# Attention and two feed-forward networks on one core: loads, conversion steps and attention in the order in which their data come, and the sigmoid ahead of the root

## The chip, the cores and the metric

One Trainium2 chip, of which the program uses one core. The metric is the device time of one execution in microseconds (us). Engines are called as the profile calls them: PE (TensorE, matrix products; PEld is its weight load), DVE (VectorE), ACT (ScalarE), POOL (GpSimd) and SP (SyncE, which here only issues transfers). All but PE's weight loads run their own instructions strictly in order, and wait for each other by semaphores.

## The reference

```python
kv  = np.einsum('bhsd,bhse->bhde', k, v)          # 4 batches, 8 heads, 576 rows, 64 wide
out = np.einsum('bhsd,bhde->bhse', q, kv)
rms = np.sqrt(np.mean(out * out, axis=-1, keepdims=True) + 1e-06)
x   = (out / rms * g_norm)                        # to 2304 x 512: tokens x (heads * 64)
gate = 1.0 / (1.0 + np.exp(-(x @ w_gate)))        # 512 x 1536
y   = (gate * (x @ w_val)) @ w_out                # 1536 x 512
h   = y @ w_in2                                   # 512 x 2048
out = (np.maximum(h, 0.0) + np.log1p(np.exp(-np.abs(h)))) @ w_out2   # 2048 x 512
```

q, k, v and g_norm are float32; the five weight matrices are float64.

## The kernel before

**Products.** A large product runs as three passes in the type float32r: both operands are split into a high and a low part, and high by high, high by low and low by high are summed in PSUM (`mm3`). So each operand needs its high part (a cast on ACT, `split_hi`, L67) and its low part (a subtraction on DVE, `split_lo`, L70), and the passes with the low parts come last.

**Stages.** The tokens are cut into five tiles of 512, 512, 384, 384 and 512. The first FFN takes tile after tile, and in each tile 12 steps of 128 columns of the hidden width: chain "g" (x by w_gate into `ps_g`), sigmoid on ACT into `sg` (`sigmoid`), chain "v" (x by w_val into `ps_v`), the gating `sg * ps_v` on DVE (`gated`), its high part on ACT and its low part on DVE (`ghl`), and the output chain of the step before into `yacc`. The second FFN takes the five tiles again, 16 steps each: `ps_h`, a softplus in pieces on ACT and DVE (`e`, `u`, `ln`, `ghl2`), and the output chain two steps later into `oacc`. The y between the two is written out and loaded again, and split for the second FFN by `y_split`.

**Attention.** For tile 0 it stands ahead of everything, one pair of heads (hp 0 to 3) after another: `kv_mm`, the transposed q (`qt_mm`), `o_mm`, the sum of squares (`o_square`), root and reciprocal (`o_root`), scaling (`o_scale`), transposition (`xt_mm`), and the split of x (`xt_split`). For tile 1 the same pieces lie in steps 2 to 8 of tile 0, and for tiles 2 to 4 (the piece being up to 256 tokens: `q_trans`, `po_mm`, `ss_mm`, `rms_root`, `rms_scale`) in the steps of the tile ahead.

**Weights.** They come as pairs of 32-bit words in loads of 512 KB; two units (a unit is what one step needs of one matrix) make an item of 1 MB. Item 0 is gate and value of step 0, item 1 the output units of steps 0 and 1, item 2 gate and value of step 1, item 3 those of step 2, item 4 the output units of steps 2 and 3, and so on: 18 items for the first FFN, 16 for the second. Each item is made into float32r by four operations: A (`conv_a`, two passes on ACT, L141 and L143), B (`conv_b`, two on DVE, L150 and L153), H (`conv_h`, ACT, L67) and L (`conv_l`, DVE, L70). `conv_step` issues H, A, B and L of up to four different items, if there is something for each; `conv_to(done)` repeats it until so many items have had L; `conv_target(n)` gives that number for each step. Items of the second FFN are loaded in the last tile of the first one, into blocks that its finished steps give free (`prefetch`); the scratch tiles of attention (`scratch`) lie in the blocks of the last seven items of the first FFN, which so can be loaded only when attention for tile 1 is done with them.

**Order.** Nothing is scheduled by a planner: the code's own order is the order of each engine. A step of the first FFN has places, at which the pieces of attention are put by a table: chain "g"; "A"; gating of the step before; "a"; its low part; "bg"; a third of the conversion; the sigmoid; chain "v"; "B"; a third; "b"; a third; the output chain; "C", "c", "late". All loads are issued by SP, at most eight under way at a time, so that a load waits there both for its place and for its block.

```python
        if ph == 1:
            done = n_l[0]
            step = max(0, conv_target(n) - done)
...
            run("bg")
...
            conv_to(done + (step + 2) // 3)
            sigmoid(t, i)
            ffn1_mm(t, i, "v", range(3 if n == 0 else 0, KD))
```

Of the kernel before, what the change touches and what calls it, by code (L numbers as in the profile page):

```python
# [8 lines left out]
F32 = mybir.dt.float32  # L9
# [20 lines left out]
def attention_moe_moe_kernel(ctx: ExitStack, tc: tile.TileContext, q, k, v, g_norm,  # L30
# [141 lines left out]

    def conv_step():
# [35 lines left out]
    QROWS, KV, QT, SQ, ON, KVF = 0, 2, (7, 8), 9, (10, 11), 12  # L211
# [398 lines left out]
    two = (nc.sync, nc.scalar)  # L610
    load_kv(0, 0, two)
# [4 lines left out]
    for hh in range(2):  # L616
        nc.scalar.dma_start(out=g_col[64 * hh:64 * hh + 64, :], in_=g_norm.rearrange("(d o) -> d o", o=1))
    load_kv(0, 2)
    load_q_rows(0, 2)
    load_item()  # L620
    load_kv(0, 3)
    load_q_rows(0, 3)

    def a_in(hp):
        kv_mm(0, hp)
        qt_mm(0, hp, MM)
        kv_evac(0, hp)
# [19 lines left out]
    conv_a()
    a_out(2)
    conv_b()
    a_x(1)  # L650
    conv_h()
    for _ in range(3):
        load_item()
    for part in (0, "rest", 1, 2, 3):
        load_kv(1, part)
    load_item()
    load_item()
    a_out(3)
    conv_l()
    for c in "gv":  # L660
        ffn1_mm(0, 0, c, (0,))
    conv_a()
    a_x(2)
    for c in "gv":
        ffn1_mm(0, 0, c, (1,))
    conv_b()
    a_x(3)
    for c in "gv":
        ffn1_mm(0, 0, c, (2,))
    conv_step()  # L670
# [17 lines left out]
    def call(f, *a):  # L688
        return lambda: f(*a)
# [60 lines left out]
    for n in range(len(its) + LAG2):  # L750
# [15 lines left out]
        if ph == 1:  # L766
# [6 lines left out]
            gate_lo_prev()  # L773
            run("bg")
# [10 lines left out]
        elif ph == 2:  # L785
# [10 lines left out]
            if n_l[0] < len(items):  # L796
                conv_step()
# [63 lines left out]
```

## Time and profile before

| | before |
|---|---|
| median of three runs | 960.85 us (960.76 to 962.49) |
| the profiled execution | 963.4 us |
| its span in the profile | 961.6 us |
| mean granted TensorE clock | 0.982 |
| busy: PE, PEld | 918.1 us (95%), 785.0 us (82%) |
| busy: DVE, ACT, POOL | 550.5 us (57%), 456.2 us (47%), 1.6 us (0%) |

The busy times are averages over stages that differ. A granted clock of 1.0 is 2.4 GHz, one of 0.5 is 1.2 GHz, at which a matmul takes twice as long. The span is the profiled execution from its first instruction to its last, and the difference to its time lies around it.

### The profile page before, as it was taken

To read this page: it belongs to the slowest core of one execution; us is meant where nothing else is said; L and a number is where in the kernel's file an instruction comes from. 1 tells how busy PE (TensorE), PEld (TensorE's weight loads), DVE (VectorE), ACT (ScalarE), POOL (GpSimd) and SP (SyncE) were. 2 spreads that over 40 slices of the span, in tenths; PEclk is the share of its full clock that TensorE was granted. 3 is DMA by queue.
4 is the path that set the end of the run, shared out by engine and by line. 5 is a ranking of instruction groups with operands and counts; after the bars stand their busy time and mean duration, and the time that the engine had idled before them with its cause. 6 is when DMAs were issued, how large, how long until landed. Compare 5 with 4: busy or idle time off the path is not lost.

```text
span 961.6 us, 11999 instructions
## 1 busy us (share of the span) xinstructions
PE 918.1 (95%) x4685; PEld 785.0 (82%) x4685; DVE 550.5 (57%) x909; ACT 456.2 (47%) x784; POOL 1.6 (0%) x8
## 2 busy tenths in 40 slices
PE   7489999999999999999989999999999999999998
PEld 6267778878898999999867768888888999998886
DVE  2656675343455534555676675566566566566554
ACT  3555755332335334442656654454445445454443
POOL 0000000000000000000000000000000000000000
PEclk9789989999999999999999999999999999999999
DMA  9760511321011302000645520002001102000001
GB/s 304 229 234 20 200 53 46 99 62 20 0 49 43 92 3 56 22 22 1 220 163 175 175 88 1 1 0 77 1 1 33 45 1 78 1 1 33 1 1 44
DMA packets 72137, 64.75 MB, mean 67 GB/s; under 512 B 30352, under 2 KB 63120, under 8 KB 72080
## 3 DMA queue, kind: packets, MB, share of 16 engines
q1 hardware_dynamic: 70848, 63.33, 21.1%
q10 hardware_dynamic: 1232, 0.66, 0.3%
q8 instruction: 37, 0.61, 0.3%
q14 instruction: 20, 0.16, 0.1%
HBM read 54.53 MB, written 9.44 MB: 67 GB/s over the span
## 4 chain that ended last, share of the span: by engine, by line
PE 80%; DMA 7%; DVE 6%; ACT 4%; issue 2%; SPq 1%; DVEq 0%; ACTq 0%
PE oacc L63 21%; PE ps_h L63 20%; PE ps_g L63 12%; PE ps_v L63 12%; PE yacc L63 11%; DMA w_raw<-in_moe_w_in_dram 2%; DVE w_raw L150 2%; DVE w L70 1%; DMA kv_raw<-in_k_dram 1%; DVE w L153 1%; DMA w_raw<-in_moe_w_gate_dram 1%; DMA kv_raw<-in_v_dram 1%; ACT w_raw L143 1%; PE kv_ps L255 1%; ACT w_raw L141 1%
## 5 line engine op out<-in xcount | busy, mean ns | idle before, releaser
L63 PE MATMUL oacc<-w,ghl 128*128 128x512 f32 x864 | 210.4, 391 | 0.0
L63 PE MATMUL ps_g<-x,w 128*128 128x512 f32 (+1 forms) x720 | 167.6, 380 | 26.2 <-ACT sg L479 13.4
L63 PEld LDWEIGHTS oacc<-w,ghl 128*128 128x128 f32 x864 | 161.5, 188 | 32.9 <-DVE ghl L70 0.8
L63 PEld LDWEIGHTS ps_g<-x,w 128*128 128x128 f32 x720 | 133.4, 193 | 49.2 <-ACT sg L479 16.0
L63 PE MATMUL ps_v<-x,w 128*128 128x512 f32 (+1 forms) x720 | 162.7, 374 | 5.9 <-DVE sg L485 5.9
L63 PE MATMUL yacc<-ghl,w 128*128 128x512 f32 (+1 forms) x720 | 161.9, 373 | 2.1 <-ACT ghl L67 1.9
L63 PEld LDWEIGHTS ps_v<-x,w 128*128 128x128 f32 x720 | 131.1, 190 | 25.5 <-DVE sg L485 8.3
L63 PEld LDWEIGHTS yacc<-ghl,w 128*128 128x128 f32 x720 | 130.8, 189 | 20.2 <-ACT ghl L67 2.3
L551 ACT ACTIVATE e<-ps_h 128x512 f32<-128x512 f32 (+1 forms) x80 | 44.4, 556 | 199.4 <-PE ps_h L63 190.2
L63 PE MATMUL ps_h<-y,w 128*128 128x512 f32 (+1 forms) x576 | 128.5, 372 | 0.3 <-ACT sg L479 0.3
L63 PEld LDWEIGHTS ps_h<-y,w 128*128 128x128 f32 x576 | 106.1, 188 | 17.1 <-ACT sg L479 0.7
L560 DVE TENSOR_SCALAR u<-e 128x512 f32<-128x512 f32 (+1 forms) x80 | 32.0, 400 | 149.4 <-ACT e L552 149.4
L63 PE MATMUL ps_h<-y_odd,w 128*128 128x512 f32 (+1 forms) x384 | 82.4, 363 | 0.0
L67 ACT CAST ghl<-sg 128x512 fp32r<-128x512 f32 (+1 forms) x60 | 34.6, 577 | 98.5 <-DVE sg L485 98.3
L63 PEld LDWEIGHTS ps_h<-y_odd,w 128*128 128x128 f32 x384 | 70.2, 188 | 8.9
L70 DVE TENSOR_TENSOR ghl<-sg,ghl 128x512 fp32r<-128x512 f32 (+1 forms) x60 | 38.2, 636 | 29.4 <-ACT ghl L67 29.2
L562 DVE SCALAR_TENSOR_TENSOR e<-ps_h,e 128x512 f32<-128x512 f32 (+1 forms) x80 | 51.0, 638 | 2.8
L569 DVE TENSOR_TENSOR e<-e,u 128x512 f32<-128x512 f32 (+1 forms) x80 | 51.0, 638 | 2.8
L70 DVE TENSOR_TENSOR ghl<-e,ghl 128x512 fp32r<-128x512 f32 (+1 forms) x80 | 50.3, 628 | 0.7 <-ACT ghl L67 0.7
L568 DVE SCALAR_TENSOR_TENSOR u<-u,ln 128x512 f32<-128x512 f32 (+1 forms) x80 | 50.5, 631 | 0.0
L150 DVE SCALAR_TENSOR_TENSOR w_raw<-w_raw 128x1024 uint32<-128x1024 uint32 x34 | 41.5, 1221 | 15.4 <-ACT w_raw L143 15.4
L485 DVE TENSOR_TENSOR sg<-sg,ps_v 128x512 f32<-128x512 f32 (+1 forms) x60 | 37.8, 629 | 20.3 <-PE ps_v L63 12.4
(87 smaller groups left out, 765.6 us busy)
## 6 DMA issues: line engine op xcount, KB each, us to landing
w_raw<-in_moe_w_out_dram SPq DMA_DIRECT2D x28, 512.0 KB, 4.7
w_raw<-in_moe_w_in_dram SPq DMA_DIRECT2D x16, 512.0 KB, 4.9
w_raw<-in_moe_w_gate_dram SPq DMA_DIRECT2D x12, 512.0 KB, 6.3
w_raw<-in_moe_w_val_dram SPq DMA_DIRECT2D x12, 512.0 KB, 7.7
out_dram<-ob SPq DMA_DIRECT2D x17, 256.0 KB, 2.4
kv_raw<-in_k_dram SPq DMA_DIRECT2D x16, 256.0 KB, 3.9
kv_raw<-in_v_dram SPq DMA_DIRECT2D x14, 256.0 KB, 4.2
y_dram<-ys SPq DMA_DIRECT2D x6, 512.0 KB, 2.8
```

The lines of the kernel that those rows point to most:

```text
L63: nc.tensor.matmul(out=ps, lhsT=lhs(a), rhs=rhs(b), start=start and n == 0, stop=stop and n == 2)
L67: nc.scalar.copy(out=hi, in_=src)
L70: nc.vector.tensor_tensor(out=lo, in0=src, in1=hi.bitcast(F32), op=ALU.subtract)
L141: nc.scalar.activation(out=hi.bitcast(F32), in_=hi.bitcast(F32), func=ACTF.Copy, scale=float(2.0 ** -112))
L143: nc.scalar.activation(out=lo, in_=lo, func=ACTF.Copy, bias=-0.5, scale=float(2.0 ** -29 * (1 - 2.0 ** -20)))
L150: nc.vector.scalar_tensor_tensor(out=lo, in0=hi, scalar=3, in1=lo, op0=ALU.logical_shift_left, op1=ALU.bitwise_or)
L485: nc.vector.tensor_tensor(out=sg, in0=sg, in1=chain.pop(("v", t, i)), op=ALU.mult)
L551: nc.scalar.activation(out=e, in_=ps, func=ACTF.Abs)
L560: nc.vector.tensor_scalar(out=u, in0=e, scalar1=1.0, scalar2=None, op0=ALU.add)
L562: nc.vector.scalar_tensor_tensor(out=e, in0=chain.pop(("p", t, i)), scalar=0.0, in1=e, op0=ALU.max, op1=ALU.add)
L568: nc.vector.scalar_tensor_tensor(out=u, in0=u, scalar=1.0, in1=ln, op0=ALU.subtract, op1=ALU.subtract)
L569: nc.vector.tensor_tensor(out=e, in0=e, in1=u, op=ALU.subtract)
```

## The change

- Item 0 is no longer converted as an item: its gate unit and its value unit are loaded, converted (A, B, H, L at half width, lines named `early_`) and used each by itself. In step 0 chain "v" stands whole behind chain "g", and no longer piece by piece beside it.
- Attention for tile 0 is issued in another order (`a_in`, `a_q`, `a_o`, `a_scale` and the transpositions apart). Items 1 to 5 are loaded ahead of k and v of batch 1, and g_norm by SP instead of ACT.
- Attention for tile 1 lies a step later in tile 0. The late loads are two in step 4, three in step 6, and two in step 9 at "bg". The scratch tiles lie in other blocks, and the last two items of the first FFN change places.
- How far the conversion goes in each step of tile 0 stands in two tables, `L_END` for L and `A_LIM` for A.
- In each step of the first FFN the first third of the conversion and the sigmoid stand ahead of "bg" (where the roots of attention are) and of `y_split`.
- In the last tile of the first FFN conversion goes one item a step and stays further behind the loads. In the second FFN what is left of it is done in every second step.
- The scalings behind a root are spread over other places, and the first piece of tile 3 lies a step later in parts.

```diff
+    for n in (n_first - 2, n_first - 1):
+        for (kind, f) in items[2 * n_first - 3 - n]:
+            block_of["gv" if kind in "gv" else "o", f] = n
+    items[-2:] = items[:-3:-1]
...
-        if na < n_load[0]:
+        if na < min(n_load[0], a_lim[0]):
             conv_a()
...
-    QROWS, KV, QT, SQ, ON, KVF = 0, 2, (7, 8), 9, (10, 11), 12
+    KV, SQ, QROWS, QT, KVF, ON = 0, 5, 6, (8, 9), 10, (12, 13)
...
+    a_in(0)
+    a_q(0)
...
+    early_a(0)
+    a_q(2)
+    xt_mm(0, 0, ACC)
+    a_scale(1)
+    early_b(0)
...
+    early_h(0)
+    xt_split(0, 1)
+    early_l(0)
+    a_o(3)
+    early_a(1)
+    ffn1_mm(0, 0, "g", (0,))
+    xt_mm(0, 2, ACC)
+    a_scale(3)
+    early_b(1)
+    xt_split(0, 2)
+    ffn1_mm(0, 0, "g", (1,))
+    early_h(1)
...
-    at_place(6, "bg", call(o_root, 1, slice(0, NP)))
+    at_place(7, "bg", call(o_root, 1, slice(0, NP)))
+    at_place(7, "late", call(o_scale, 1, 0), call(o_scale, 1, 1))
+    at_place(8, "bg", call(o_scale, 1, 2), call(o_scale, 1, 3))
+    at_place(8, "late", call(kvb_split))
...
+    for n, c, m in ((4, "late", 2), (6, "late", 3), (9, "bg", 2)):
+        at_place(n, c, *[load_item] * m)
...
+            if n + 1 < len(ps) and TILES1[u - 1][1] < 512 and m > 160:
+                when = ((1, "bg"), (2, "bg"), (3, "bg"), (4, "bg"))
+            else:
+                when = ((1, "bg"), (1, "late"), (2, "bg"), (2, "late"))
...
+    A_LIM = (4, 6, 6, 7, 9, 11, 13, 14, 16, 16, 18, 18)
+    L_END = (3, 5, 6, 7, 9, 10, 12, 13, 15, 16, 18, 18)
...
-        if n < n1 - F1:
-            return min(n_first, (3 * n + 4) // 2 + 1)
-        return min(len(items), n_first + max(0, (n - (n1 - F1) - 1) * 3 // 2))
+        i = n - (n1 - F1)
+        if i < 0:
+            a_lim[0] = A_LIM[min(n, F1 - 1)]
+            return L_END[min(n, F1 - 1)]
+        a_lim[0] = n_first + max(0, i - 1 + max(0, i - 2) // 2)
+        return n_first + max(0, i - 2)
...
             gate_lo_prev()
+            conv_to(done + (step + 2) // 3)
+            sigmoid(t, i)
             run("bg")
             if t == NT1 - 1 and i < 2:
                 y_split(0, 2 * i)
                 y_split(0, 2 * i + 1)
-            conv_to(done + (step + 2) // 3)
-            sigmoid(t, i)
-            ffn1_mm(t, i, "v", range(3 if n == 0 else 0, KD))
+            ffn1_mm(t, i, "v")
...
-            if n_l[0] < len(items):
+            if n_l[0] < len(items) and i % 2 == 0:
+                a_lim[0] = len(items)
                 conv_step()
```

**ACT, up to the first sigmoid.** On ACT the last rows up to the first sigmoid (`sg`) were these before; `w_raw` is an item under A, `w32` to `w` with 128x2x512 is its H, and `x<-xT` the split of x. Lines of the kernel changed are six higher than the same lines before.

```order
L372 ACTIVATE x_251<-xT_366,g_col_83 128x512
L67 CAST w_379<-w32_364 128x2x512
L141 ACTIVATE w_raw_304<-w_raw_304 128x1024
L143 ACTIVATE w_raw_304<-w_raw_304 128x1024
L141 ACTIVATE w_raw_307<-w_raw_307 128x1024
L143 ACTIVATE w_raw_307<-w_raw_307 128x1024
L67 CAST w_432<-w32_430 128x2x512
L141 ACTIVATE w_raw_323<-w_raw_323 128x1024
...
L479 ACT_TABLE_LOAD
```

Now they are these, where `w_raw0` is a unit of item 0 alone:

```order
L628 ACTIVATE w_raw0_152<-w_raw0_152 128x512
L629 ACTIVATE w_raw0_152<-w_raw0_152 128x512
...
L67 CAST w_312<-w_raw0_152 128x512
L378 ACTIVATE x_271<-xT_346,g_col_83 128x512
L145 ACTIVATE w_raw_154<-w_raw_154 128x1024
...
L145 ACTIVATE w_raw_157<-w_raw_157 128x1024
...
L67 CAST w_420<-w32_418 128x2x512
L145 ACTIVATE w_raw_160<-w_raw_160 128x1024
...
L485 ACT_TABLE_LOAD
L485 ACTIVATE sg_428<-ps_g_326 128x512
```

Before, three A and two H of full width stand behind the last split of x, and the A, H and A ahead of them stand among the splits; now three A and one H stand behind the last split, and the work among the splits is at half width.

**DVE, steps 7 and 8 of tile 0.** On DVE, behind the root for tile 1, these rows stood before, from the reciprocal to the next gating; `on` is the scaling, `sg` the gating, `w_raw` and `w32` are B, `w` is L.

```order
L350 RECIPROCAL stat_772<-stat_773 128x32
L150 SCALAR_TENSOR_TENSOR w_raw_778<-w_raw_778 128x1024
L153 SCALAR_TENSOR_TENSOR w32_890<-w_raw_778 128x1024
L70 TENSOR_TENSOR w_885<-w32_818,w_885 128x2x512
L150 SCALAR_TENSOR_TENSOR w_raw_781<-w_raw_781 128x1024
L153 SCALAR_TENSOR_TENSOR w32_913<-w_raw_781 128x1024
L70 TENSOR_TENSOR w_908<-w32_890,w_908 128x2x512
L355 TENSOR_TENSOR on_776<-on_776,stat_772 128x512 x2
L70 TENSOR_TENSOR kvb_108<-kvf_110,kvb_108 128x512
L485 TENSOR_TENSOR sg_893<-sg_893,ps_v_895 128x512
```

Now these rows stand there, a step later, from the scalings to the L that the gate chain behind them needs:

```order
L361 TENSOR_TENSOR on_838<-on_838,stat_834 128x512 x2
L491 TENSOR_TENSOR sg_958<-sg_958,ps_v_962 128x512
L70 TENSOR_TENSOR ghl_1008<-sg_958,ghl_1008 128x512
L154 SCALAR_TENSOR_TENSOR w_raw_927<-w_raw_927 128x1024
L157 SCALAR_TENSOR_TENSOR w32_1016<-w_raw_927 128x1024
L154 SCALAR_TENSOR_TENSOR w_raw_930<-w_raw_930 128x1024
L157 SCALAR_TENSOR_TENSOR w32_1023<-w_raw_930 128x1024
L70 TENSOR_TENSOR w_1018<-w32_1016,w_1018 128x2x512
L361 TENSOR_TENSOR on_838<-on_838,stat_834 128x512 x2
L154 SCALAR_TENSOR_TENSOR w_raw_933<-w_raw_933 128x1024
L157 SCALAR_TENSOR_TENSOR w32_1051<-w_raw_933 128x1024
L70 TENSOR_TENSOR w_1048<-w32_1023,w_1048 128x2x512
```

Three B, two L and two scalings stand between this gating and the next one; before, it was two B, two L and two scalings.

**DVE, start of the second FFN.** Before, behind the last gating of the first FFN, one L was left, and no B; `ys` is the copy of y, `u` and `e` are softplus.

```order
L485 TENSOR_TENSOR sg_4462<-sg_4462,ps_v_4464 128x512
L70 TENSOR_TENSOR ghl_4496<-sg_4462,ghl_4496 128x512
L70 TENSOR_TENSOR w_4521<-w32_4480,w_4521 128x2x512
L560 TENSOR_SCALAR u_4527<-e_4524 128x512
L562 SCALAR_TENSOR_TENSOR e_4524<-ps_h_4508,e_4524 128x512
```

Now a B and an L stand there, and again two steps later, and so on, the last L in step 12:

```order
L491 TENSOR_TENSOR sg_4428<-sg_4428,ps_v_4430 128x512
L70 TENSOR_TENSOR ghl_4456<-sg_4428,ghl_4456 128x512
L154 SCALAR_TENSOR_TENSOR w_raw_4229<-w_raw_4229 128x1024
L157 SCALAR_TENSOR_TENSOR w32_4486<-w_raw_4229 128x1024
L70 TENSOR_TENSOR w_4481<-w32_4425,w_4481 128x2x512
L566 TENSOR_SCALAR u_4492<-e_4489 128x512
L568 SCALAR_TENSOR_TENSOR e_4489<-ps_h_4468,e_4489 128x512
...
L154 SCALAR_TENSOR_TENSOR w_raw_4284<-w_raw_4284 128x1024
L157 SCALAR_TENSOR_TENSOR w32_4563<-w_raw_4284 128x1024
L70 TENSOR_TENSOR w_4558<-w32_4486,w_4558 128x2x512
L566 TENSOR_SCALAR u_4571<-e_4566 128x512
```

Ahead of the gating, the B, B, L, B, L that followed one another in the last step before have become one B and one L a step.

## Rows read from the trace of the kernel before

**Rows 1.** The page's busy times: engine, us, share of the span, instructions.

```profile
PE 918.1 (95%) x4685; PEld 785.0 (82%) x4685; DVE 550.5 (57%) x909; ACT 456.2 (47%) x784; POOL 1.6 (0%) x8
```

**Rows 2.** Timeline of PE, 50 to 70 us: start, us, instruction, idle before.

```profile
51.23 5.09 PE L63 MATMUL ps_g<-x,w 128*128 128x512 f32 x12 [8.78 <-ACT sg L479]
...
64.41 0.95 PE L255 MATMUL kv_ps<-kv_raw 128*64 128x64 f32 x20
65.29 3.01 PE L63 MATMUL ps_v<-x,w 128*128 128x512 f32 x12
```

**Rows 3.** Three windows: us, then busy PE, PEld, DVE, ACT, POOL; PEclk; DMA.

```profile
42.00:51.00 9.00, 0.46 (x2) 0.02 (x1) 6.66 (x6) 8.45 (x9) 0.00 (x0) 0.69 0.26 64
120.60:127.40 6.80, 6.20 (x15) 4.85 (x16) 6.08 (x10) 5.44 (x8) 0.00 (x0) 0.50 0.00 0
560.90:564.30 3.40, 3.40 (x9) 2.63 (x8) 2.08 (x3) 2.86 (x5) 0.00 (x0) 0.50 0.02 5
```

**Rows 4.** PE's waits, 42 to 165 us: us in total, times, longest.

```profile
PE ps_g L63 <- DVE w L70: 2.1, 3, 1.0
PE ps_g L63 <- ACT w L67: 2.0, 1, 2.0
```

**Rows 5.** PE's waits, 165 to 440 us.

```profile
PE ps_v L63 <- DVE sg L485: 2.3, 3, 1.2
PE ps_g L63 <- ACT sg L479: 2.0, 3, 0.9
PE kv_ps L255 <- DMA kv_raw<-in_v_dram: 0.7, 1, 0.7
```

**Rows 6.** PE's waits, 440 to 570 us.

```profile
PE ps_v L63 <- DVE sg L485: 3.6, 4, 1.1
PE ps_g L63 <- ACT sg L479: 2.6, 3, 1.2
PE yacc L63 <- ACT ghl L67: 1.9, 1, 1.9
PE ps_h L63 <- ACT sg L479: 0.3, 1, 0.3
PE yacc L63 <- DVE ghl L70: 0.2, 1, 0.2
```

**Rows 7.** DVE by line and form, 0 to 60 us: busy us, mean ns; idle before.

```profile
L150 DVE SCALAR_TENSOR_TENSOR w_raw<-w_raw 128x1024 uint32<-128x1024 uint32 x5 | 6.1, 1220 | 0.8 <-ACT w_raw L143 0.8
L70 DVE TENSOR_TENSOR w<-w,w 128x1024 fp32r<-128x1024 f32 x4 | 4.9, 1218 | 0.5 <-ACT w L67 0.5
```

**Rows 8.** ACT by line and form, 0 to 60 us.

```profile
L141 ACT ACTIVATE w_raw<-w_raw 128x1024 f32<-128x1024 f32 x6 | 7.0, 1160 | 0.0
L67 ACT CAST w<-w 128x1024 fp32r<-128x1024 f32 x4 | 4.2, 1046 | 3.8 <-DVE w L153 3.8
```

**Rows 9.** The chain that ended last, 0 to 60 us: start, us, what.

```profile
10.23 7.51 DMA kv_raw<-in_v_dram
```

**Rows 10.** Timeline of SP's queue, 25 to 60 us.

```profile
33.12 17.71 SPq L287 DMA_DIRECT2D q_rows<-in_q_dram  x24
```

**Rows 11.** The page's DMA issues: count, KB each, median us to landing.

```profile
w_raw<-in_moe_w_out_dram SPq DMA_DIRECT2D x28, 512.0 KB, 4.7
```

**Rows 12.** Timeline of all engines, 394 to 407 us, around a root.

```profile
395.51 1.28 ACT L451 ACT_TABLE_LOAD   x1
...
397.98 1.28 ACT L479 ACT_TABLE_LOAD   x1
...
400.85 1.75 DVE L457 RECIPROCAL ms<-ms 128x256 f32<-128x256 f32 x1
```

**Rows 13.** The page's groups of the second FFN.

```profile
L551 ACT ACTIVATE e<-ps_h 128x512 f32<-128x512 f32 (+1 forms) x80 | 44.4, 556 | 199.4 <-PE ps_h L63 190.2
...
L560 DVE TENSOR_SCALAR u<-e 128x512 f32<-128x512 f32 (+1 forms) x80 | 32.0, 400 | 149.4 <-ACT e L552 149.4
...
L562 DVE SCALAR_TENSOR_TENSOR e<-ps_h,e 128x512 f32<-128x512 f32 (+1 forms) x80 | 51.0, 638 | 2.8
```

More of the change, by code (lines that the diff above doesn't have):

```diff
@@ L171, in conv_l @@
         n_l[0] += 1
+    a_lim = [0]
     def conv_step():
@@ L610, in attention_moe_moe_kernel, with early_load, early_a, early_b @@
     two = (nc.sync, nc.scalar)
+    early = {}
+    def early_load(j):
+        unit, w = src_of["gv"[j]]
+        early[j] = t = stage.tile([P, 512, 2], U32, tag="st", name="w_raw0")
+        nc.sync.dma_start(out=t.rearrange("p c two -> p (c two)").rearrange("p (k m) -> p k m", k=KD), in_=unit(w, 0))
+    def early_a(j):
+        lo, hi = early[j][:, :, 0], early[j][:, :, 1]
+        nc.scalar.activation(out=hi.bitcast(F32), in_=hi.bitcast(F32), func=ACTF.Copy, scale=float(2.0 ** -112))
+        nc.scalar.activation(out=lo, in_=lo, func=ACTF.Copy, bias=-0.5, scale=float(2.0 ** -29 * (1 - 2.0 ** -20)))
+    def early_b(j):
+        lo, hi = early[j][:, :, 0], early[j][:, :, 1]
+        nc.vector.scalar_tensor_tensor(out=lo, in0=hi, scalar=3, in1=lo,
+                                       op0=ALU.logical_shift_left, op1=ALU.bitwise_or)
+        nc.vector.scalar_tensor_tensor(out=lo, in0=hi, scalar=0x80000000, in1=lo,
+                                       op0=ALU.bitwise_and, op1=ALU.bitwise_or)
+    def early_h(j):
+        if j == 0:
+            early["w"] = block(dst[0], [P, 2, 2, 512], F32R, "w")
+        W["gv"[j], 0] = early["w"][:, j]
+        split_hi(early["w"][:, j, HI], early[j][:, :, 0].bitcast(F32))
+    def early_l(j):
+        split_lo(early["w"][:, j, LO], early[j][:, :, 0].bitcast(F32), early["w"][:, j, HI])
+    for n in (n_load, n_a, n_b, n_h, n_l):
+        n[0] = 1
     load_kv(0, 0, two)
@@ L615, in attention_moe_moe_kernel, with a_q, a_o, a_scale @@
     load_q_rows(0, 1)
-    for hh in range(2):
-        nc.scalar.dma_start(out=g_col[64 * hh:64 * hh + 64, :], in_=g_norm.rearrange("(d o) -> d o", o=1))
+    early_load(0)
     load_kv(0, 2)
     load_q_rows(0, 2)
-    load_item()
+    for hh in range(2):
+        nc.sync.dma_start(out=g_col[64 * hh:64 * hh + 64, :], in_=g_norm.rearrange("(d o) -> d o", o=1))
     load_kv(0, 3)
     load_q_rows(0, 3)
+    early_load(1)
+    for _ in range(5):
+        load_item()
     def a_in(hp):
         kv_mm(0, hp)
+        kv_evac(0, hp)
+    def a_q(hp):
         qt_mm(0, hp, MM)
-        kv_evac(0, hp)
         qt_evac(0, hp)
-    def a_out(hp):
+    def a_o(hp):
         o_mm(0, hp, ACC)
         o_square(0, hp)
+    def a_scale(hp):
         o_root(0, slice(hp, hp + 1))
         o_scale(0, hp)
-    def a_x(hp):
-        xt_mm(0, hp, ACC)
-        xt_split(0, hp)
     a_in(0)
+    a_q(0)
     a_in(1)
-    a_out(0)
+    a_o(0)
+    a_q(1)
+    a_scale(0)
     a_in(2)
-    a_out(1)
-    a_x(0)
-    a_in(3)
[L647 to L653, printed above, removed]
+    a_o(1)
+    early_a(0)
[3 more added lines that the diff above has]
+    early_b(0)
+    xt_split(0, 0)
+    a_in(3)
+    a_o(2)
+    a_q(3)
+    xt_mm(0, 1, ACC)
+    a_scale(2)
+    early_h(0)
[10 more added lines that the diff above has]
+    early_h(1)
+    xt_mm(0, 3, ACC)
+    xt_split(0, 3)
+    early_l(1)
+    ffn1_mm(0, 0, "g", (2,))
     for part in (0, "rest", 1, 2, 3):
         load_kv(1, part)
[L656 to L670, printed above, removed]
     for hp in range(NP):
```

16 lines of the change are left out of this document (7 added, 9 removed).

## The prediction

> **What bounds the kernel now.** I read the page first: TensorE (PE) is busy 95% of the span [rows 1], so the change can only win where PE idles or runs at its lower clock. Then PE's own waits, stage by stage, and the clock by stretches. There are five stages. Up to 51.23 us the start: PE waits 8.8 us for the first sigmoid [rows 2], and ACT is busy 8.45 of the 9 us ahead of it, mostly converting weights, so ACT's order sets the start [rows 3]. In the rest of the first tile PE waits 2.0 + 2.1 us for converted weights [rows 4], and behind the longest of these waits the granted clock is 0.50 for 6.8 us, 1.2 instead of 2.4 GHz: 3.4 us lost [rows 3]. In tiles 1 to 3 it waits 5.0 us, mostly behind roots [rows 5]. In the last tile and at the border to the second FFN it waits 8.6 us: 3.6 and 2.6 for the sigmoid and what hangs on it, 1.9 and two small ones at the border [rows 6], and the clock is 0.50 for 3.4 us there, 1.7 us lost [rows 3]. From 565 us on nothing waits.
>
> **The start.** In the letters of the code, A is two ACT passes of some 1.15 us over a 1 MB item, B two DVE passes of 1.22, H one ACT cast of 1.05, L one DVE subtraction of 1.22 [rows 7, 8]. Before, A, B, H and L of all of item 0 stand among the attention steps, and four more A and two H stand ahead of the first sigmoid. The change puts gate and value of item 0 through alone, at half width (each pass half as long and a little, 0.6 to 0.7 us), and moves chain "v" behind chain "g". Walked through the new order with these durations and 0.05 us from engine to engine:
> the second head pair's v lands at 12.4 (an estimate: before it landed some 1.4 us earlier, and a 512 KB gate unit now goes ahead of it; the landings of this stretch follow each other at about 1.5 us per 512 KB). Its products, the square, A of the gate, the next q copy and the root end at 17.2. From there DVE works with hardly a pause: reciprocal, scale, B, lo of x, two kv copies, sum, scale, lo, L, sum, scale, B of the value unit, two lo, L: 30.4. ACT then does A of items 1, 2 and 3, one H and the table load (28.9 + 3 x 2.25 + 1.05 + 0.4 of waiting + 1.28): sigmoid at 38.2 to 38.8, where before it was at 50.6 to 51.2. H and L of item 2 end at 39.8 and 41.0, so the second gate chain runs from 39.8, with its low pass from 41.0. One thing is late next: B of items 3 to 5 and L stand on DVE ahead of the second gating, which ends at 52.7, so the value chain of step 2 begins at 53.0. Before it begins at 65.29, behind one attention product of 0.88 that the change has not done by then [rows 2]: **-11.4 us**. Bounds: the whole walk hangs on landings that I moved by hand; v of the fourth pair took 7.5 us to land before [rows 9]. 3 us either way.
>
> **The rest of the first tile.** The 24 q loads hold SP for 17.7 us, from 33.12 [rows 10], before and after, because the bytes ahead of them are the same; items 6 to 10 are then issued near 50.5 and the gate of step 4 lands near 54 to 56, its A is wanted near 57: no wait. Attention for tile 1 starts one step later. The new crowd is on DVE. Step 6: ACT comes out of square, copy and H at 2.2 us after the value chain starts, A at 4.4, sigmoid, A at 7.1; DVE does B, B, L by 10.8; PE is through its 8.0 us and two passes at 8.6: 2.4 us of waiting (0.25 and 0.7 in steps 4 and 5 by the same walk). Step 7: A of item 13 stands ahead of the sigmoid; its load is released by the last sum of squares, 12.0, and takes about 4.7 us [rows 11]: sigmoid at 19.5, PE ready at 18.5: 1.0. Behind it the root, reciprocal and two scalings end at 22.7 ahead of the gating: 0.75. Step 8: behind that gating DVE has B, B, L, two scalings, B, L = 2.45 + 2.45 + 1.2 + 1.3 + 2.45 + 1.2 = 11.0 us, all ahead of the next gate chain's low pass, while PE has 6.2 us and two passes: it waits 2.2 for the scaled rows, 1.4 for sigmoid and H, 1.9 for L, together 5.5. Sum 10.6, against 4.1 before. I add 2.0 for the clock (the stretch of 6 us with hardly a matmul ends in the lower clock, as at 121; the drop that step 6's wait may bring is hidden, because DVE sets the end), against 3.4: **+5.1 us**. Bounds: 3.3 us of waiting in step 8 if the load of item 13 is early, and none or 6.8 us of the lower clock.
>
> **Sigmoid ahead of the root.** At 395.51 a root brings table load, root and table load, 1.28 + 1.19 + 1.28 us, ahead of the sigmoid that PE waits for, and a reciprocal, 1.75 us, ahead of the gating costs PE up to 1.2 more [rows 5, 12]. After, root and first load stand behind the sigmoid, where PE has the value chain, the old output chain and the next gate chain ahead of it (6 us at 384 columns); the second load stands behind the gating's cast, under the same cover. Seven roots; of the 5.0 us in tiles 1 to 3 [rows 5] I leave 0.5: **-4.5 us**. If the cover fails, it stays at 0. The Trainium skill, page "ScalarE: Activation LUTs", section "What ACT_TABLE_LOAD costs", gives about 2.66 us for a switch of tables, a drain of 1.38 included; each row has 1.28, and the 1.19 between the two loads is the root's own time, so the rows decide. By the Trainium skill's figure seven pairs would give back up to 19.3 us more, and the sum would be 925.4.
>
> **Last tile.** Before, A of an item just loaded stands ahead of the sigmoid and waits for its landing. The new targets convert one item per step, one or two steps later: per 8.16 us ACT has ghl, H, A, sigmoid = 4.4 and DVE gating, lo, B, L = 5.0, and each load has a whole step (8 us, against some 5 of landing). Nothing is late next: **-6.2 us** for the two waits of [rows 6]. At the border the gating is no longer behind B, B and L: **-4.1 us** (2.4 of waiting, 1.7 of clock).
>
> **Second FFN.** Here the change pays: before, every item is converted but for one L when it begins; after, seven are left, one every second step. Per step DVE has 0.40 and four of about 0.64 = 3.0 us, ACT four of 0.56 to 0.63 [rows 13]. In a step with conversion DVE has 3.0 + 3.6 = 6.6 of 5.44 us, over two steps 9.6 of 10.9: it fits, but in order. Walked from the last value chain's end at 0: A of item 28 ends at 5.9, B and L on DVE at 9.5, then two y copies; the first output chain gets its hi at 13.8 and its lo at 14.8 where PE asks at 13.6 and 14.3: 0.8 us. Step 2: H and A on ACT until 17.5, B and L on DVE until 21.2, lo of step 1 only at 22.9, where PE asks at 20.3: 2.6 us. From step 4 on DVE has caught up and the same chain costs 0.3 at each of four steps. With about an even chance of a fall of the clock behind the 2.6 us (0.5 x 1.7): 0.8 + 2.6 + 1.2 + 0.9, taken as **+5.0 us** (before, nothing). Bounds 1 and 12.
>
> The rest costs nothing: g_norm's loads moved from ACT to SP are two tiny ones, due at 17; the swap of the last two items only changes blocks; the y casts behind the sigmoid lie in the slack of the last tile; the extra step in tile 3 may remove the one wait for a load, 0.7, which is in the 5.0.
>
> **Sum:** -11.4 + 5.1 - 4.5 - 6.2 - 4.1 + 5.0 = -16.1. The profiled execution took 963.4 us for its span of 961.6, so 947.3 for its like; it is 2.6 above the median of the runs shown (960.85), so **944.7 us** for a median.
>
> **Rivals.**
> 1. The crowds of step 8 and of the second FFN dissolve, because DVE is further ahead than I walked: +5.1 and +5.0 become about 0: 934.6. For it: I chained every wait in one order, and an engine that is early anywhere breaks it. Against: 11.0 us of DVE work behind one gating needs no wait to be late.
> 2. The start wins only half, because A of item 3, which needs its landing near 27, and DVE's walk slip by 5 to 6 us: about 950.4. For: the granted clock is 0.69 in the start's last 9 us [rows 3], and every product of attention is longer when it falls. Against: ACT and DVE set the walk.
> 3. The sigmoid's move does nothing: the load before the next sigmoid comes as late as the pair did: 949.2. Against: 6 us of cover.
> 4. Slower: each of the seven conversions in the second FFN costs what I give to the second, 2.6 us, and the clock falls each time, 1.7: 30 instead of 5, 969.8. It ends above the old time from 3.0 us for each, since (16.1 + 5.0) / 7 = 3.0. For: 6.6 us of DVE in a step of 5.44. Against: two steps have 1.3 us to spare.
>
> **Chances.** My forecast, 939 to 951: 0.56. Rival 1, 932 to 939: 0.22. Rivals 2 and 3 beyond that band or together, 951 to 957: 0.17. Rival 4: 0.04, and 0.01 for no change. 0.2%, 1.9 us, is about what this measurement can tell from none. Range: 934 to 954, which leaves out the ends of rivals 1 and 2 and all of 4. Faster 0.95, same 0.01, slower 0.04.
>
> **What would show it.** The first sigmoid near 39 us and step 2's value chain near 53; PE waits of about 2 us in step 6 and several in step 8, near 130, for DVE's scaled rows and L, and a lower clock there; no sigmoid behind a pair of loads; no wait for a landing on ACT in the last tile; one wait near 2.6 us for lo in the second FFN's step 2, and small ones behind. A first sigmoid past 44 us, or waits at each conversion of the second FFN, would make it wrong.

## The result, and the profile after

The kernel after takes 936.93 us (median of four runs, 936.52 to 937.49), the kernel before 961.67 (four runs beside them, 960.76 to 964.09): a ratio of 0.974, 95% interval 0.972 to 0.976, so 24.7 us faster, 23.1 to 27.0 by the interval. The forecast was 944.7, with a range of 934 to 954. The profiled execution has a span of 935.7 us where before it had 961.6; the lines of the page with the busy times and with PE's clock in 40 slices now read

```profile
PE 909.8 (97%) x4685; PEld 780.6 (83%) x4685; DVE 550.2 (59%) x912; ACT 457.1 (49%) x787; POOL 1.6 (0%) x8
...
PEclk9899989999999999999999999999999999999999
```

The work is the same, 4685 instructions. Of the 25.9 us of span, 17.6 are idle time of PE; the other 8.3 are busy time, as less of PE's work falls into stretches at the lower clock (mean granted clock 0.993, before 0.982). The table gives where the 25.9 us came from, read from the starts of the same chain of PE in the two timelines (a chain is the 12 matmuls of one product). "Earlier by" is the difference so far, the next column what the stretch itself adds to it. The profile of before lies 1.7 us above the median of its kernel and that of after 0.6, so the medians differ by 24.7.

| stretch, up to the start of | before | after | earlier by | the stretch | forecast |
|---|---|---|---|---|---|
| the output chain of step 0 | 58.88 | 46.88 | 12.0 | -12.0 | -11.4 |
| the output chain of tile 1's first step | 182.08 | 175.23 | 6.9 | +5.1 | +5.1 |
| the output chain of tile 3's last step | 454.26 | 440.48 | 13.8 | -6.9 | -4.5 |
| the output chain of the last tile's step 10 | 551.76 | 529.66 | 22.1 | -8.3 | -6.2 |
| step 3 of the second FFN | 573.24 | 546.25 | 27.0 | -4.9 | -4.1 |
| the end | 961.61 | 935.70 | 25.9 | +1.1 | +5.0 |

The forecast's +5.0 for the second FFN holds 0.8 us for its first output chain, which stands ahead of step 3 and so in the stretch of the border.

**The start.** The timeline of ACT and PE around the first sigmoid, to be held against [rows 2]:

```profile
36.66 1.28 ACT L485 ACT_TABLE_LOAD   x1
37.96 0.60 ACT L485 ACTIVATE sg<-ps_g 128x512 f32<-128x512 f32 x1
38.45 1.04 ACT L67 CAST w<-w 128x1024 fp32r<-128x1024 f32 x1
39.54 4.76 PE L63 MATMUL ps_g<-x,w 128*128 128x512 f32 x12 [5.03 <-ACT w L67]
...
52.32 2.88 PE L63 MATMUL ps_v<-x,w 128*128 128x512 f32 x12
```

The sigmoid stands at 37.96 (forecast 38.2), the second gate chain at 39.54 (39.8), the value chain of step 2 at 52.32 (53.0). PE still waits 5.0 us there, now for H of item 2 behind the sigmoid.

**The rest of the first tile.** PE's waits from 42 to 165 us, the counterpart of [rows 4], and behind them none at all from 165 to 440 us, where [rows 5] had 5.0; then the one wait from 440 us on, the counterpart of [rows 6]:

```profile
PE ps_g L63 <- DVE w L70: 4.0, 3, 1.8
PE xT L367 <- DVE on L361: 1.8, 1, 1.8
PE ps_g L63 <- ACT w L67: 1.2, 1, 1.2
PE ps_g L63 <- ACT sg L485: 0.7, 1, 0.7
PE ps_v L63 <- DVE sg L491: 0.5, 1, 0.5
...
PE oacc L63 <- DVE ghl L70: 0.8, 1, 0.8
```

Two stages wait longer than before: the first tile, 8.2 us against 4.1, and the second FFN, the 0.8 us of the last line, against nothing. The crowd of step 8 is where the forecast put it, as the timeline of DVE and PE shows; the window under it has the granted clock behind it at 0.50, as the second of [rows 3] had:

```profile
127.81 1.29 DVE L361 TENSOR_TENSOR on<-on,stat 128x512 f32<-128x512 f32 x2
128.64 0.63 PE L367 MATMUL xT<-kvf,on 128*128 128x128 f32 x4 [1.77 <-DVE on L361]
...
131.41 1.22 DVE L70 TENSOR_TENSOR w<-w,w 128x1024 fp32r<-128x1024 f32 x1
...
132.69 4.64 PE L63 MATMUL ps_g<-x,w 128*128 128x512 f32 x10 [1.48 <-DVE w L70]
```

```profile
131.60:138.40 6.80, 5.71 (x15) 4.59 (x16) 2.92 (x4) 1.30 (x3) 0.00 (x0) 0.50 0.01 2
```

**A wait's price.** Three chains of the last tile in the timeline of PE, first before, then after:

```profile
495.89 2.88 PE L63 MATMUL yacc<-ghl,w 128*128 128x512 f32 x12
499.53 3.02 PE L63 MATMUL ps_g<-x,w 128*128 128x512 f32 x12 [0.76 <-ACT sg L479]
503.30 3.02 PE L63 MATMUL ps_v<-x,w 128*128 128x512 f32 x12 [0.76 <-DVE sg L485]
```

```profile
480.70 2.88 PE L63 MATMUL yacc<-ghl,w 128*128 128x512 f32 x12
483.42 2.88 PE L63 MATMUL ps_g<-x,w 128*128 128x512 f32 x12
486.14 2.88 PE L63 MATMUL ps_v<-x,w 128*128 128x512 f32 x12
```

A chain of 12 is shown as 2.88 us long, but the next one starts 2.72 us behind its start: 0.16 of its last matmul lies under the next chain's first (the profile models where matmuls end; starts are what is compared here). Behind a wait that overlap is gone, and the chain is longer (3.02 instead of 2.88). From 499.53 to 503.30 are 3.77 us, so a wait shown as 0.76 costs 1.05: 0.29 more than the idle time shown. The seven waits of the last tile, compared one by one with the same chains of after, cost 0.28 to 0.31 more each.

### The profile page after: what moved, and what is told of

The parts are those of the page before. It is cut to its first block, busy times and chain, and to the rows that moved or that the text cites. A ratio compares the mean times of both kernels' runs of the same rounds, so it can differ in the third digit from the quotient of the medians.

```text
span 935.7 us, 11996 instructions
## 1 busy us (share of the span) xinstructions
PE 909.8 (97%) x4685; PEld 780.6 (83%) x4685; DVE 550.2 (59%) x912; ACT 457.1 (49%) x787; POOL 1.6 (0%) x8
## 4 chain that ended last, share of the span: by engine, by line
PE 88%; DVE 4%; DMA 3%; ACT 3%; issue 1%; SPq 0%; ACTq 0%; DVEq 0%
PE oacc L63 21%; PE ps_h L63 21%; PE ps_g L63 15%; PE yacc L63 14%; PE ps_v L63 14%; DMA kv_raw<-in_v_dram 1%; PE kv_ps L261 1%; DMA w_raw<-in_moe_w_out_dram 1%; DVE w_raw L154 1%; PE po L63 1%; DVE w L70 1%; DVE w L157 1%; ACT w_raw L145 1%; ACT w_raw L147 1%; DMA kv_raw<-in_k_dram 1%
## 5 line engine op out<-in xcount | busy, mean ns | idle before, releaser
L63 PE MATMUL ps_v<-x,w 128*128 128x512 f32 (+1 forms) x720 | 160.6, 372 | 0.5 <-DVE sg L491 0.5
L63 PE MATMUL yacc<-ghl,w 128*128 128x512 f32 (+1 forms) x720 | 159.7, 370 | 0.0
L70 DVE TENSOR_TENSOR ghl<-sg,ghl 128x512 fp32r<-128x512 f32 (+1 forms) x60 | 38.2, 636 | 23.5 <-ACT ghl L67 23.4
L567 ACT ACTIVATE ln<-u 128x512 f32<-128x512 f32 (+1 forms) x80 | 47.3, 591 | 6.9 <-DVE u L566 6.0
L485 ACT ACTIVATE sg<-ps_g 128x512 f32<-128x512 f32 (+1 forms) x60 | 33.3, 556 | 35.3 <-PE ps_g L63 35.2
```

The source lines that it names most:

```text
L63: nc.tensor.matmul(out=ps, lhsT=lhs(a), rhs=rhs(b), start=start and n == 0, stop=stop and n == 2)
L70: nc.vector.tensor_tensor(out=lo, in0=src, in1=hi.bitcast(F32), op=ALU.subtract)
L485: nc.scalar.activation(out=sg, in_=chain.pop(("g", t, i)), func=ACTF.Sigmoid)
L567: nc.scalar.activation(out=ln, in_=u, func=ACTF.Ln)
```

## The experiments

In each profile the stretches of the table are compared with those of the kernel from which it was made; times are medians, ratios are to the kernel before, run on the same chip.

**Sigmoid ahead of the root, alone.** In the kernel before:

```diff
+            conv_to(done + (step + 2) // 3)
+            sigmoid(t, i)
             run("bg")
...
-            conv_to(done + (step + 2) // 3)
-            sigmoid(t, i)
```

> The kernel before with one part of the change: in each step of the first FFN the first third of the conversion and the sigmoid stand ahead of the roots and of y_split. Theory 1 (a wait of PE costs 0.28 us more than the idle time shown beside it, since matmuls overlap in a chain and the overlap is lost): the six waits behind roots in tiles 1 to 3 show 4.3 us and give back 4.3 + 6 x 0.28 = 6.0 us; the 0.7 us of waiting for a load stays; 955.0 against 961. Theory 2 (the idle time shown is the price): 4.3 us, 956.7. Theory 3 (the load of the sigmoid's table now comes as late as the pair did): less than 2 us.

957.30 against 962.45, ratio 0.995 (0.993 to 0.997). In tiles 1 to 3 PE still has these waits:

```profile
PE ps_v L63 <- DVE sg L485: 1.2, 3, 0.6
PE kv_ps L255 <- DMA kv_raw<-in_v_dram: 0.7, 1, 0.7
```

So 3.1 of the 5.0 us of [rows 5] went, and the stretch became 3.9 us shorter (182.08 to 454.26 before, 180.94 to 449.21 here). Three waits are gone for good: 0.8 / 3 = 0.27 beside each, the price that theory 1 has; by that of theory 2, the 3.1 us that went would have been all. The sums of both, 6.0 and 4.3, were too high, because the three waits for the gating stay: reciprocal and first scaling still stand ahead of it on DVE. Theory 3 falls. (The time fell by more, 5.2 us. Tile 0 behind the start is 1.4 us shorter in this profile, with 3.4 us at the lower clock instead of 6.8, but so it is in the run with the targets alone, whose first tile is that of before.)

**The scalings at their old places.** In the kernel after:

```diff
-            if n + 1 < len(ps) and TILES1[u - 1][1] < 512 and m > 160:
-                when = ((1, "bg"), (2, "bg"), (3, "bg"), (4, "bg"))
-            else:
-                when = ((1, "bg"), (1, "late"), (2, "bg"), (2, "late"))
+            when = ((0, "late"), (1, "bg"), (1, "late"), (2, "bg"))
```

> The kernel after, with the four scalings behind each root in tiles 1 to 3 spread as before (the first at the end of the root's own step). Theory 1 (the reciprocal and the first scaling stood ahead of the gating, and their place, not only the root's, made PE wait): waits for the gating of 0.2, 0.6 and 0.4 us come back in tiles 1 to 3, with 0.28 beside each 2.0 us. Theory 2 (once the root stands behind the sigmoid nothing is left): no change.

939.98 us (two runs). Two of the three waits come back:

```profile
PE ps_v L63 <- DVE sg L491: 1.0, 2, 0.6
```

Tiles 1 to 3 are 1.8 us longer. Compared chain by chain with after, these two waits, 0.57 and 0.41, cost 0.86 and 0.68 us, so 0.29 and 0.27 more than shown. At the third gating PE idles only 0.05, too little for this list, and still loses 0.12, since the overlap is used up first; the last 0.14 appears at a chain without idle time. Theory 1. The gain in tiles 1 to 3 is thus 3.9 for the sigmoid's place and 1.8 for the scalings'; the remaining 1.2 of the 6.9 is not tried apart. The wait of 0.7 for a load, which is not there any more, would be 1.0 of it at the same price.

**The conversion's targets, alone.** In the kernel before:

```diff
-        return min(len(items), n_first + max(0, (n - (n1 - F1) - 1) * 3 // 2))
+        i = n - (n1 - F1)
+        a_lim[0] = n_first + max(0, i - 1 + max(0, i - 2) // 2)
+        return n_first + max(0, i - 2)
...
-            if n_l[0] < len(items):
+            if n_l[0] < len(items) and i % 2 == 0:
+                a_lim[0] = len(items)
                 conv_step()
```

> The kernel before with one part of the change: the conversion's targets in the last tile of the first FFN, and in the second FFN one step of conversion in every second step. Theory 1 (0.28 us more than the idle time for each wait removed): last tile 6.2 + 7 x 0.28 = 8.2, border 4.9, second FFN 1.1 back, together 12.0 us, 949. Theory 2 (idle time and clock as shown): 6.2 + 4.1 - 0.8 = 9.5 us, 951.5. Theory 3 (the forecast's second FFN, 5.0 us back): 5.3 us, 955.7.

950.21 against 962.45, ratio 0.988 (0.986 to 0.991). From 440 us on the only wait left is

```profile
PE oacc L63 <- DVE ghl L70: 0.8, 1, 0.8
```

and the stretches read -8.3, -4.9 and +1.1: 12.1 in all, theory 1 to 0.1 us in each. Theory 1 had its 0.28 from the profile of after, so what is new here is that this part of the change alone makes what is gained in the last tile and at the border and lost in the second FFN.

Of the border's 4.9, 1.5 us are not the change's in every execution: the run with the transpositions (below), which has the code of before from step 1 on, shows no lower clock there, and its stretch is 19.9 us long where that of before has 21.5.

```profile
555.00:566.00 11.00, 8.84 (x36) 6.79 (x37) 8.57 (x12) 6.63 (x10) 0.00 (x0) 1.00 0.01 2
```

**B behind the A of its own step.** In the kernel after, in the second FFN:

```diff
-                a_lim[0] = len(items)
-                conv_step()
+                if n_h[0] < n_b[0]:
+                    conv_h()
+                if i > 0 and n_a[0] < len(items):
+                    conv_a()
+                if n_b[0] < n_a[0]:
+                    conv_b()
+                if n_l[0] < n_h[0]:
+                    conv_l()
```

> The kernel after, but in the second FFN A is left out of step 0 and comes two steps later for each item, so that B in every step waits for the A issued in the same step, as the forecast's walk had it. Theory 1 (the forecast was wrong there because B works on an item whose A was done two steps before, and so stands on DVE without waiting): in step 2 the low part of step 1 now comes at about 551.0 where PE asks at 549.6; a wait of 2.1 us instead of 0.78, the second FFN 1.3 to 1.6 us longer, nothing at the later conversions. Theory 2 (DVE's amount of work sets it): the same 0.78. Theory 3 (each conversion costs the same): 2 us at each of six steps.

938.08 us (two runs). First the timeline of the kernel after (L of step 0, then step 2 of the second FFN), then that of this kernel:

```profile
534.32 1.22 DVE L70 TENSOR_TENSOR w<-w,w 128x1024 fp32r<-128x1024 f32 x1
...
543.97 1.14 ACT L145 ACTIVATE w_raw<-w_raw 128x1024 f32<-128x1024 f32 x1
...
545.02 1.17 ACT L147 ACTIVATE w_raw<-w_raw 128x1024 uint32<-128x1024 uint32 x1
545.03 1.22 DVE L154 SCALAR_TENSOR_TENSOR w_raw<-w_raw 128x1024 uint32<-128x1024 uint32 x1
...
547.43 1.22 DVE L70 TENSOR_TENSOR w<-w,w 128x1024 fp32r<-128x1024 f32 x1
...
549.63 0.68 DVE L70 TENSOR_TENSOR ghl<-e,ghl 128x512 fp32r<-128x512 f32 x1
...
550.36 2.57 PE L63 MATMUL oacc<-w,ghl 128*128 128x512 f32 x10 [0.78 <-DVE ghl L70]
```

```profile
543.52 1.14 ACT L145 ACTIVATE w_raw<-w_raw 128x1024 f32<-128x1024 f32 x1
...
545.70 1.23 DVE L154 SCALAR_TENSOR_TENSOR w_raw<-w_raw 128x1024 uint32<-128x1024 uint32 x1 [1.04 <-ACT w_raw L147]
...
550.30 0.68 DVE L70 TENSOR_TENSOR ghl<-e,ghl 128x512 fp32r<-128x512 f32 x1
...
551.04 2.60 PE L63 MATMUL oacc<-w,ghl 128*128 128x512 f32 x10 [1.91 <-DVE ghl L70]
```

After, B starts 1.06 us behind the start of A in the same step, since it works on an item whose A was done earlier. Chained, DVE idles 1.04 us for A, and PE waits 1.91; the second FFN is 1.2 us longer, and no later conversion costs anything. Theory 1. (Here B follows its own A from step 2 on, so the wait of 0.8 us that the forecast had in step 0 is not tried.)

**A held back in the start.** In the kernel before, `conv_step` takes A only for items below 3 until the first sigmoid is issued:

```diff
-        if na < n_load[0]:
+        if na < min(n_load[0], a_lim[0]):
...
+            a_lim[0] = 3 if n == 0 else 99
             conv_to(done + (step + 2) // 3)
             sigmoid(t, i)
+            a_lim[0] = 99
```

> The kernel before, with A of items 3 and 4 held back until the first sigmoid has been issued. Theory 1 (ACT's order sets the first sigmoid): A of item 4, 2.25 us, stands between H of item 2 and the table load, and goes; A of item 3 is hidden behind B of item 2; the first sigmoid comes 2.2 us sooner, near 48.4, and the time falls by 2 us, to 959, if nothing behind it is late for the two A. Theory 2 (the loads set the start): no change, 961.

959.02 against 962.45, ratio 0.997 (0.995 to 0.998). PE's wait for the first sigmoid fell from 8.78 to 6.61 us, by 2.2: theory 1. (The profiled start is 4.1 us earlier; the rest of that lies in earlier landings and a shorter stretch at the lower clock, which the order of A does not reach.)

**The transpositions first.** In the kernel before:

```diff
     a_out(3)
+    a_x(2)
+    a_x(3)
     conv_l()
...
-    a_x(2)
...
-    a_x(3)
```

> The kernel before, with the last two transpositions of x (and their splits) issued ahead of the first gate and value chains instead of between their pieces. Theory 1 (in the start ACT idles 3.2 and 2.2 us because these two stand on PE behind chains that wait for H and L of item 0): the first sigmoid comes about 5 us sooner, near 45.5, and the time is 956. Theory 2 (H and L of item 0, and nothing else, set the start): no change, 961.

960.27 against 962.45, ratio 0.998 (0.997 to 1.000). Two rows of ACT:

```profile
39.49 1.04 ACT L67 CAST w<-w 128x1024 fp32r<-128x1024 f32 x1 [2.61 <-DVE w L153]
...
49.69 0.60 ACT L479 ACTIVATE sg<-ps_g 128x512 f32<-128x512 f32 x1
```

Theory 1 fell: the splits of x are done 5 us sooner, but the sigmoid only 0.9, since A of item 1 now stands behind both splits and starts 3.6 us later (34.74 instead of 31.17). ACT's idle time moved to between this A and H of item 1, where it waits for B.

**Item 0 converted whole, and the load order by itself.** In the kernel after, first the value unit's load ahead of the fourth pair's k, v and q; then also its A, B, H and L directly behind those of the gate unit:

```diff
     load_q_rows(0, 2)
+    early_load(1)
...
-    early_load(1)
```

```diff
     early_a(0)
+    early_a(1)
...
     early_b(0)
+    early_b(1)
```

> The kernel after, with the value unit of step 0 loaded ahead of k, v and q of the fourth pair of heads instead of behind them (as the item stood before). Theory 1 (from 18 us on the order on DVE sets the start, and the fourth pair's products are taken from PSUM there only at 20.25): v lands near 16.6 instead of 15.05, and the gate chain of step 1 moves by less than 0.5 us. Theory 2 (the landing of the fourth pair sets the start): 1.5 us later.

> As the run with the value unit loaded early, and A, B, H and L of the value unit each stand directly behind those of the gate unit, as if item 0 were converted whole. Theory 1 (the sum of ACT's work up to the first sigmoid sets it, and that sum stays): the first gate chain starts 2 to 3 us later, but the sigmoid and the gate chain of step 1 move by less than 1 us. Theory 2 (the gate unit alone is what brings the sigmoid forward): both 2.6 us later.

The load order alone: 937.79 us (two runs). In its profile all of the start is 1.9 us later, but that begins ahead of the edit, at the first q, which landed at 9.42 instead of 7.71; and the fourth pair's products wait for nothing:

```profile
9.56 1.09 PE L316 MATMUL qt<-kvf,q_rows 128*64 128x128 f32 x16 [1.86 <-DMA q_rows<-in_q_dram]
...
18.36 0.95 PE L261 MATMUL kv_ps<-kv_raw 128*64 128x64 f32 x20
```

So this order is worth nothing that shows: theory 1 there. Item 0 whole: 939.90, ratio 0.977 (0.974 to 0.979), 2.5 us above the kernel after by the ratios, whose intervals overlap. With the first q landing at 7.82,

```profile
40.21 0.60 ACT L485 ACTIVATE sg<-ps_g 128x512 f32<-128x512 f32 x1
...
41.79 3.76 PE L63 MATMUL ps_g<-x,w 128*128 128x512 f32 x7 [6.39 <-ACT w L67]
```

sigmoid and gate chain are 2.25 us later. Theory 2: the sum of ACT's work is not what sets the sigmoid, the order is; the value unit's passes among the attention steps delay what stands behind them (the fourth pair's `o_mm` waits 2.26 us for DVE's copy of kv, where after it waits 0.78).

**A of item 3 behind the sigmoid.** In the kernel after:

```diff
-    A_LIM = (4, 6, 6, 7, 9, 11, 13, 14, 16, 16, 18, 18)
+    A_LIM = (3, 6, 6, 7, 9, 11, 13, 14, 16, 16, 18, 18)
```

> The kernel after, with A of item 3 behind the first sigmoid instead of ahead of it (A_LIM of step 0 is 3, not 4). Theory 1 (ACT works without a pause from 28.7 us to the first sigmoid, so its order sets it): sigmoid at 35.7 instead of 38.0 and the gate chain of step 1 at 37.3 instead of 39.5; 2.2 us off, 934.7, if item 3 is still in time for step 2. Theory 2 (given back at step 2, since H and L of item 3 come later): 0 to 0.5 us off.

937.10 us, ratio 0.973 (0.971 to 0.976): the same as after. The output chain of step 0 starts 1.9 us earlier, that of step 1 only 0.1:

```profile
48.08 3.02 PE L63 MATMUL ps_g<-x,w 128*128 128x512 f32 x12 [0.24 <-ACT sg L485]
...
51.29 0.68 DVE L491 TENSOR_TENSOR sg<-sg,ps_v 128x512 f32<-128x512 f32 x1
52.03 3.06 PE L63 MATMUL ps_v<-x,w 128*128 128x512 f32 x12 [0.93 <-DVE sg L491]
```

B and L of item 3 now stand on DVE between the two gatings. Theory 2: the value chain of step 2 is set by the sum on DVE.

**The crowd of tile 0.** Three kernels from the kernel after: attention for tile 1 and the late loads one step earlier; that with new tables; the new tables alone (in which the entries for steps 7 and 9 differ, since the late items land later).

```diff
-    at_place(7, "bg", call(o_root, 1, slice(0, NP)))
+    at_place(6, "bg", call(o_root, 1, slice(0, NP)))
...
-    for n, c, m in ((4, "late", 2), (6, "late", 3), (9, "bg", 2)):
+    for n, c, m in ((3, "late", 2), (5, "late", 3), (8, "bg", 2)):
```

```diff
-    A_LIM = (4, 6, 6, 7, 9, 11, 13, 14, 16, 16, 18, 18)
-    L_END = (3, 5, 6, 7, 9, 10, 12, 13, 15, 16, 18, 18)
+    A_LIM = (4, 6, 6, 9, 11, 13, 13, 14, 15, 17, 18, 18)
+    L_END = (3, 5, 6, 7, 10, 12, 13, 14, 15, 16, 18, 18)
```

> The kernel after, with attention for tile 1 and the late loads one step earlier (steps 2 to 8, as they lay before); the conversion's tables unchanged. Theory 1 (the waits of steps 6 to 9, 8.2 us, and the lower clock behind them come from attention and late conversion falling on the same steps): the scaled rows come a step sooner and the sigmoid of step 7 no longer waits for the landing of item 13; 2.4 us of waits and the 0.28 beside each go, 3 us; the wait for L of item 11 (1.8) and those for L of the last items stay, since the tables stay. Theory 2 (the tables alone set the waits): no change.

> As the run with attention a step earlier, and the tables spread the conversion over the steps in which DVE has room: one to three items in each of steps 3 to 5, one in each of steps 6 to 9. Theory 1: no step has three B between two gatings; the waits of steps 6 to 9 (8.2 us and 0.28 for each) and the lower clock (2.9 us) go but for 2 or 3 us, so 8 to 10 us off, 927 to 929. Theory 2 (the sum of work on DVE and ACT in tile 0 sets it, wherever it lies): the waits reappear in steps 3 to 5; less than 3 us off.

> The kernel after, attention at its own places, with the conversion's tables alone spread over the steps that have room (three items in step 4, two in step 5, none in step 7, two in step 8). Theory 1 (it is the tables, and the attention's earlier place gives nothing of its own): the wait for L of item 11 ahead of step 7 (1.8 us) and one B of the crowd in step 8 go; 3 to 5 us off, 932 to 934. Theory 2 (both are needed, since the late items land too late for the spread tables): less than 1 us off.

Attention earlier: 942.94, ratio 0.980 (0.979 to 0.982), 6 us slower than the kernel after, 4.2 of them in tile 0 behind the start. Both theories fell: waits add up to 10.5 us, and there are two stretches of 6.8 us with a granted clock of 0.50, from 113.7 and from 137.6. The root now falls into step 6, in which two items are converted, and its table load, an A and a B stand ahead of the H for which PE waits:

```profile
106.78 1.28 ACT L355 ACT_TABLE_LOAD   x1
...
108.30 1.16 ACT L145 ACTIVATE w_raw<-w_raw 128x1024 f32<-128x1024 f32 x1
...
111.21 1.05 ACT L67 CAST w<-w 128x1024 fp32r<-128x1024 f32 x1 [0.71 <-DVE w L157]
...
112.31 0.73 PE L63 MATMUL ps_g<-x,w 128*128 128x512 f32 x2 [3.41 <-ACT w L67]
```

With new tables: 934.26, ratio 0.972 (0.970 to 0.974); the profiled execution is the fastest of four, with the shortest span of all, 930.9. Tile 0 behind the start is 5.35 us shorter than in the kernel after, and no stretch behind 44 us has the lower clock. Its waits:

```profile
PE xT L367 <- ACT sg L485: 2.4, 1, 2.4
PE ps_v L63 <- DVE sg L491: 1.7, 1, 1.7
PE ps_g L63 <- ACT sg L485: 1.5, 1, 1.5
PE ps_g L63 <- DVE w L70: 0.9, 1, 0.9
```

The tables alone: 934.83, ratio 0.972 (0.971 to 0.974), tile 0 behind the start 3.0 us shorter, with one wait of 3.6 us in step 8 and the lower clock there still. So theory 1 of the second run holds for the lower clock and not for the waits, of which 6.5 of 8.2 us stay, though in four places instead of seven. Theory 1 of the last run holds for the waits that it names (the 1.8 us for L are gone, step 8 has 3.6 instead of 4.5), but others of 1.5 and 0.7 us came, and the time lies above its 932 to 934. The intervals of both overlap that of the kernel after; that they beat it is read from tile 0 in one profile of each, 123.0 and 125.3 us, where five profiles with the first tile of after have 127.0 to 128.4.

## Why the prediction was right, and where it was off

The forecast was 7.8 us too high. It lies in the range, but outside the band of 939 to 951 that it called its own. The profiles gained 9.8 us more than its sum (it took 2.6 us off for a profile above its median, and that of after is only 0.6 above). Of these the start has 0.6, the waits of tiles 1 to 3, the last tile and the border have 5.3, and the second FFN has 3.9.

**Start**: right, 12.0 for 11.4; the walk met the sigmoid, H and the value chain of step 2 within 0.7 us. One step of it did not happen: that chain does not stand behind the gating, which ended at 51.88, but directly behind its gate chain. The doubt about landings was justified, but in another place: not the fourth pair's v, whose order is worth nothing that shows, but the first loads, which moved the whole start by 1.9 us in one profile. The 12.0 us are not fully taken apart: the halves of item 0 are worth 2.25, and the new order of attention and loads, the bulk, is not tried by itself.

**Rest of the first tile**: +5.1 as forecast, in part by luck. The walked waits came, each smaller: 1.8 us for 2.4 behind step 6, 1.1 for 1.75 in step 7, 4.5 for 5.5 in step 8, none of the 0.95 in steps 4 and 5, and one of 0.7 ahead of step 11 that was not walked. That is 8.2 us where 10.6 were walked, so 4.1 more than before and not 6.5; three waits more than before, at 0.28 each, add 0.8; and the lower clock lasts 6.8 us as before, where the forecast had 1.4 us less of loss. Other pairs of profiles with the same two first tiles give from +3.8 to +6.6. Rival 1's crowd of step 8 did not dissolve.

**Tiles 1 to 3 and last tile**: the mechanism was right, the terms "-4.5" and "-6.2" were mis-sized: they take the idle time shown as the price, and the 14 waits cost 0.28 and 0.30 more each in the mean of the two stages. That is 4.0 of the 4.5 us by which the two terms were off; the remaining 0.5 is the allowance left in tiles 1 to 3, where no wait is left. The border's 0.8 more is its three waits' share; its 1.7 for the clock was right for the profile of before, and absent from two of four profiles with the same border.

The Trainium skill's 2.66 us for a switch of tables (page "ScalarE: Activation LUTs", section "What ACT_TABLE_LOAD costs") is not borne out here: the load at 36.66 starts 0.01 us behind the end of the pass ahead of it, takes 1.28 us, and the sigmoid stands at 37.96, 0.02 us behind it. No drain shows on either side.

**Second FFN**: the step that failed. "A of item 28 ends at 5.9, B and L on DVE at 9.5" put B behind the A issued in the same step. It works on the item before, so DVE was done 3.6 us sooner (at 535.54, 5.9 us behind the last value chain's end), the first of the two waits was not there, and that in step 2 was 0.78, not 2.6. The run with B chained shows how much of it is this error: a wait of 1.91 instead of 0.78. The rest goes with A of step 2, which ended 16.5 us behind the value chain's end (at 546.19) and not 17.5. The 1.2 us for four later waits and the 0.9 for the clock (the four parts add up to 5.5, taken as 5.0) did not come either, nor did they with B chained (the granted clock from 545 to 553 us is 1.00).

So that the time came out near rival 1's 934.6 is luck: one half of it, the second FFN, happened, and the other did not; the rest is the price of waits. Rivals 2 and 3 did not happen, nor did rival 4: no conversion behind the second costs anything.

## What to carry to other kernels

Price a wait of PE by the starts of two neighbouring chains, with and without it, and not by the idle time beside it: here it is 0.27 to 0.31 us more for each wait that shows, and 0.12 were lost where next to nothing showed. When walking an order by hand, write beside every operation which item it works on; a pipeline of steps waits for the step before, not for its neighbour in the same call. And where work of two kinds shares steps, move both tables together: in tile 0 of one profile each, attention a step earlier lost 4 us with the old tables and won 2 beside the new ones.

## What the hardware showed that was not expected

The start differs between executions of the same code by up to 3.7 us: in the run with the new targets alone, which has the order of before up to 440 us, PE waited 4.84 us for the fourth pair's v (the load of [rows 9]), where it waited 2.50 in the profile of before, and the output chain of step 0 came 3.7 us later. Twenty-one runs of the kernel before span 958.3 to 965.2 us. Stretches counted from a chain behind the start agree better, where neither waits nor the lower clock differ: tiles 1 to 3 are 265.25 us long in eight profiles of after and of kernels made from it. So they, and not the totals, tell changes of 1 us apart there. In tile 0 and at the border they do not, for the same code spreads by 1.3 to 1.5 us.

The lower clock did not come at the same place in kernels whose first tile is the same. After, it was granted for 6.83 us from 131.6; in the run with item 0 whole, for 3.41 us from 111.2 and 3.41 from 135.1, and tile 0 behind the start was 1.3 us shorter there. The runs with B chained and with the scalings at their old places have the same two short stretches and 127.0 and 127.1 us. In these three PE does not show the waits of 0.67 and 0.47 us for sigmoid and gating that after has behind step 7.
